# One of twelve blocks of w2 laid as four 16-row blocks on 32 partitions and loaded by eight four-row transfers, in a one-token transformer block

## The chip, the cores and the metric

One core of a Trainium2 chip runs the kernel. The metric is the device time of one execution in microseconds (us), given as the median of several runs. All times inside the execution count from the start of the profiled span.

## The reference, cut to what matters

One token x (640 values) goes through a transformer block whose layer norms are modulated by a condition c: attention over a cache of 8192 positions with 32 heads of 192, then a feed-forward part with squared ReLU.

```python
mod = silu(c) @ w_mod                      # 6 vectors: sa, ca, ga, sb, cb, gb
h = layernorm(x) * (1 + ca) + sa
x = x + ga * attention(h)                  # wq, k_cache, v_cache, wo
h = layernorm(x) * (1 + cb) + sb
r = relu(h @ w1 + b1) ** 2                 # 1536 values
x = x + gb * (r @ w2 + b2)                 # w2: 1536 x 640
```

Everything is 32-bit float. The caches hold nearly all of the 452 MB that are read.

## The kernel before, in words

The kernel streams HBM through three large buffers, each 128 partitions by 14208 floats (`slot`). For each head h, `load_k` brings the keys, with a piece of wq or wo behind them in the same transfer, and `load_v` brings the values. VectorE (DVE) multiplies the keys by the query (`keys`, L201) and sums the products with GpSimd's help (L203 to L205), `softmax` turns the scores into weights, and TensorE (PE) applies them to the values (`values`, L240). A new transfer is issued when the buffer that it overwrites has been used.

Behind the last head come the weights of the rest, all issued by SyncE (SP), whose queue issues in the order of the program: the second part of wm1 (L312), w1 in two pieces (L315), gb, which is the last sixth of w_mod (L316), and w2 in five pieces (`W2_CUT`, L319). w1 and gb share one buffer and take the place of the last head's keys. w2 takes another buffer, that of the last head's values, so it can be issued once PE has applied them. w2 has 1536 rows: they lie as 12 blocks, each of 128 partitions by 640 columns (`FB = 12`); the pieces hold 6, 3, 1, 1 and 1 blocks.

Every transfer signals its landing on one of eight semaphores, DMAHW0 to DMAHW7, which are dealt out in turn along the program. An issue that takes a semaphore whose earlier transfer isn't known to have landed waits for that landing first, and the queue behind it waits with it.

The end of the program is one chain: `project`, `attend` and the second layer norm give hT2; 20 matmuls (L343) make ps_f from w1; DVE adds the bias, applies ReLU and squares (L346 to L348) and transposes the result to fT; 20 matmuls make mods from gb; `WARM = 2` rounds of four matmuls whose result nobody reads follow (L355); then 48 matmuls (L363) sum fT with w2 into ps_y, one block after another as the pieces land; DVE multiplies and adds (L366, L367) and SP stores out_y (L368). A 32-bit matmul appears as two matmul and two weight-load records in the profile, so these 48 matmuls are 96 pairs there.

At the start, `spread` lays the biases out for DVE (L88, L90) while PE computes the first query.

Of the kernel before, what the change touches and what calls it, by code (L numbers as in the profile page):

```python
# [8 lines left out]
F32 = mybir.dt.float32  # L9
# [4 lines left out]
P = 128  # L14
D = 640
# [3 lines left out]
FF = 1536  # L19
G = 4  # L20
DG = D // G
FG = FF // G
KB = DG // 32
FB = FG // 32
PW = 2 * DH
E = 8
ED = 64
# [9 lines left out]
WITHOUT_W = (1, H - 2)  # L37
WITH_W = tuple(h for h in range(H) if h not in WITHOUT_W)
W1_CUT = ((0, 3), (3, 2))
W2_CUT = ((0, 6), (6, 3), (9, 1), (10, 1), (11, 1))  # L40
WARM = 2
EPS = 1e-5


@with_exitstack
def block_kernel(ctx: ExitStack, tc: tile.TileContext, kw, ky, vc, wm0, wm1, w1, gb, w2, out):
    nc = tc.nc
    const = ctx.enter_context(tc.tile_pool(name="const", bufs=1))
    strm = ctx.enter_context(tc.tile_pool(name="strm", bufs=3))
    work = ctx.enter_context(tc.tile_pool(name="work", bufs=2))  # L50
# [3 lines left out]
    def slot(name):  # L54
        return strm.tile([P, SLOT], F32, tag="slot", name=name, bufs=3)
# [16 lines left out]
    wm0_t = slot("wm0_t")  # L72
    nc.sync.dma_start(wm0_t[:, :wm0.shape[1]], wm0)

    small = const.tile([P, 2 * KB + FB + KB], F32, name="small")
    nc.vector.tensor_copy(small, wm0_t[:, KB * 2 * D + WQ:wm0.shape[1]])  # L76
    x_c, c_c, bbc = small[:, :KB], small[:, KB:2 * KB], small[:, 2 * KB:]

    def columns(src, n, name, pool=const, **how):

        t = pool.tile([P, n // 32, 32], F32, name=name, **how)
        nc.vector.transpose(t.rearrange("p b r -> p (b r)"), src)
        return t

    def spread(src, n, name):

        t = work.tile([P, FB + KB, 32], F32, name=name + "_c", tag="spread", bufs=1)
        nc.vector.tensor_copy(t[:, :n], src[:, :, None].to_broadcast([P, n, 32]))  # L88
        r = const.tile([P, 32 * n], F32, name=name)
        nc.vector.transpose(r, t[:, :n].rearrange("p b r -> p (b r)"))  # L90
        return r
# [38 lines left out]
    mods = const.tile([P, 6, DG], F32, name="mods")  # L130
# [144 lines left out]
    def gather():  # L275
# [3 lines left out]
        for g in range(G):  # L279
            nc.tensor.matmul(att_t[0][32 * g:32 * (g + 1), :DG], ident[:, 32 * (g // 2):32 * (g // 2) + 1].to_broadcast([P, 32]),  # L280
                             att_s[:, DG * (g % 2):DG * (g % 2 + 1)], start=True, stop=False)

    x_t = spread(x_c, KB, "x_t")
    bbt = spread(bbc, FB + KB, "bbt")
    for h in range(H):
        i = h // 2
        if h:
# [18 lines left out]
        p = softmax(h, sc)  # L306
# [4 lines left out]

    nc.sync.dma_start(wm1_t[:, WO + KB * D:WO + KB * 3 * D], wm1[:, WO + KB * D:])  # L312
    w1_t = slot("w1_t")
    for b0, n in W1_CUT:
        nc.sync.dma_start(w1_t[:, b0 * FF:(b0 + n) * FF], w1[:, b0 * FF:(b0 + n) * FF])  # L315
    nc.sync.dma_start(w1_t[:, KB * FF:KB * (FF + D)], gb)  # L316
    w2_t = slot("w2_t")
    for b0, n in W2_CUT:
        nc.sync.dma_start(w2_t[:, b0 * D:(b0 + n) * D], w2[:, b0 * D:(b0 + n) * D])  # L319
    gb_t = w1_t[:, KB * FF:KB * (FF + D)].rearrange("p (b n) -> p b n", b=KB)  # L320
    w1_t = w1_t[:, :KB * FF].rearrange("p (b n) -> p b n", b=KB)
    w2_t = w2_t[:, :FB * D].rearrange("p (b n) -> p b n", b=FB)

    project(NPAIR - 1)
# [25 lines left out]

    next(mod(5, 1, gb_t))
    idle = psum.tile([P, 512], F32, tag="sm", name="ps_warm", bufs=2)
    for k in range(WARM):
        for g in range(G):
            nc.tensor.matmul(idle[32 * g:32 * (g + 1)], ones[:, :32], w1_t[:, k, :512], start=True, stop=True)  # L355
    gb2 = const.tile([P, DG], F32, name="gb2")
    nc.vector.tensor_mul(gb2, mods[:, 5], bbt[:, FG:])
    nc.vector.tensor_add(x1, x1, gb2)

    py = psum.tile([P, 512], F32, tag="q", name="ps_y", bufs=2)  # L360
    for b in range(FB):
        for g in range(G):
            nc.tensor.matmul(py[32 * g:32 * (g + 1), :DG], fT[:, b], w2_t[:, b, DG * g:DG * (g + 1)],  # L363
                             start=(b == 0), stop=(b == FB - 1))
    y = const.tile([P, DG], F32, name="y")
    nc.vector.tensor_mul(y, py[:, :DG], mods[:, 5])  # L366
    nc.vector.tensor_add(y, y, x1)  # L367
# [43 lines left out]
```

## Time and profile before

| what | value |
|---|---|
| median of 3 runs | 1057.85 us (1057.68 to 1058.02) |
| profiled execution | 1057.63 us |
| its span | 1055.8 us |
| DVE busy | 831.4 us (79%) |
| PE busy | 451.2 us (43%) |
| GpSimd (POOL) busy | 194.7 us (18%) |
| ScalarE (ACT) busy | 33.4 us (3%) |
| HBM read | 451.82 MB, mean 428 GB/s over the span |
| mean granted TensorE clock | 0.696 of full speed |

Read it from the bottom up: the 16 DMA engines are busy in nine tenths or more of nearly every slice of the span, while no compute engine is. "SPq" in a row means SP's queue: the time of an issue is what SP spends on it, and the data land later.

### The profile page before, as it was taken

How to read it: one execution, taken by the hardware profiler on the slowest of the kernel's cores; microseconds unless marked ns; L12 is line 12 of the kernel's file. 1: busy time of each engine (PE TensorE's matmuls, PEld its weight loads, DVE VectorE, ACT ScalarE, POOL GpSimd, SP SyncE). 2: the span in 40 equal slices, each digit the busy share in tenths (PEclk: the TensorE clock that was granted, in tenths of full speed). 3: DMA queues.
4: the chain of work that ended last, by engine and by line, in shares of the span. 5: the costliest groups of instructions: out<-in, count | busy, mean ns of one | idle time of the engine just before them, and what ended most of it. 6: DMA issues, size and time to landing. Idle time of an engine off the chain costs nothing.

```text
span 1055.8 us, 5623 instructions
## 1 busy us (share of the span) xinstructions
PE 451.2 (43%) x2324; PEld 143.5 (14%) x2324; DVE 831.4 (79%) x409; ACT 33.4 (3%) x88; POOL 194.7 (18%) x72
## 2 busy tenths in 40 slices
PE   3235443344543344363334534335453334545446
PEld 1101111011111111020111111101111111111113
DVE  2886878978787987878888687987878798789963
ACT  1000000000000000000000000000000000000000
POOL 0211112211212221212221212221211221122110
PEclk9667656776665777666577666666666676666769
DMA  9999999999999999999999999999999999999997
GB/s 403 439 434 424 436 436 426 443 424 435 433 435 426 442 424 439 431 433 426 435 432 439 428 436 427 434 437 433 428 435 430 431 436 432 433 429 431 426 423 306
DMA packets 11409, 452.18 MB, mean 428 GB/s; under 512 B 1268, under 2 KB 1272, under 8 KB 1784
## 3 DMA queue, kind: packets, MB, share of 16 engines
q1 hardware_dynamic: 11384, 451.83, 99.3%
q8 instruction: 18, 0.29, 0.1%
q14 instruction: 7, 0.06, 0.0%
HBM read 451.82 MB, written 0.00 MB: 428 GB/s over the span
## 4 chain that ended last, share of the span: by engine, by line
DMA 42%; DVE 39%; PE 17%; ACT 1%; issue 1%; SPq 0%; DVEq 0%; ACTq 0%
DMA k<-in_kw 36%; DVE k L201 21%; PE ps_o L240 14%; DVE sc L204 12%; DVE sc L205 5%; DMA k<-in_ky 3%; DMA w_t<-in_w 2%; DMA wm_t<-in_wm 1%; ACT p L228 1%; PE ps_sum L97 1%; PE ps_mx L220 1%; PE ps_mod L140 1%; PE ps_q L181 0%; DVE nm L222 0%; DVE mp L218 0%
## 5 line engine op out<-in xcount | busy, mean ns | idle before, releaser
L201 DVE TENSOR_TENSOR k<-k,qb 128x6144 f32<-128x6144 f32 (+1 forms) x66 | 419.7, 6359 | 152.3 <-DMA k<-in_kw 148.0
L203 POOL TENSOR_TENSOR k<-k 128x1344 f32<-128x1344 f32 (+1 forms) x66 | 194.0, 2940 | 821.0 <-DVE k L201 443.9
L240 PE MATMUL ps_o<-v,p 128*32 128x512 f32 x1536 | 291.9, 734 | 17.2 <-ACT p L228 17.2
L204 DVE TENSOR_REDUCE sc<-k 128x18 f32<-128x3456 f32 (+1 forms) x66 | 240.5, 3644 | 4.3
L220 PE MATMUL ps_mx<-ident,mp 128*128 128x128 f32 x32 | 15.2, 474 | 421.7 <-DVE mp L218 421.7
L267 PE MATMUL att_a<-k,oT 128*32 128x320 f32 x180 | 49.5, 719 | 118.3 <-DVE oT L262 117.1
L205 DVE TENSOR_REDUCE sc<-k 128x14 f32<-128x1344 f32 (+1 forms) x66 | 99.0, 1500 | 0.0
L240 PEld LDWEIGHTS ps_o<-v,p 128*32 128x32 f32 x1536 | 68.7, 132 | 216.6 <-issue 194.3
L220 PEld LDWEIGHTS ps_mx<-ident,mp 128*128 128x128 f32 x32 | 5.8, 182 | 448.2 <-DVE mp L218 427.2
L181 PE MATMUL ps_q<-k,hR 128*128 128x384 f32 x150 | 52.4, 496 | 1.7 <-DMA k<-in_kw 1.7
L228 ACT ACTIVATE p<-sc,nm 128x256 f32<-128x256 f32 x32 | 16.2, 508 | 759.9 <-DVE nm L222 496.4
L267 PEld LDWEIGHTS att_a<-k,oT 128*32 128x32 f32 x180 | 13.7, 161 | 140.8 <-DVE oT L262 120.7
L181 PEld LDWEIGHTS ps_q<-k,hR 128*128 128x128 f32 x150 | 27.3, 190 | 29.9 <-issue 14.0
L254 DVE SCALAR_TENSOR_TENSOR om<-ps_o,r,mask 96x512 f32<-96x512 f32 x32 | 23.9, 747 | 7.0 <-PE ps_o L240 5.8
L222 DVE TENSOR_REDUCE nm<-ps_mx 128x1 f32<-128x128 f32 x32 | 9.3, 292 | 18.2 <-PE ps_mx L220 18.2
L256 DVE TENSOR_REDUCE os<-om 96x64 f32<-96x512 f32 x32 | 21.8, 682 | 1.1
L97 PE MATMUL ps_sum<-sp,ones 128*128 128x2 f32 x32 | 9.4, 364 | 17.2 <-ACT p L228 17.2
L140 PE MATMUL ps_mod<-wm_t,silu 128*32 128x320 f32 (+1 forms) x120 | 10.5, 503 | 14.5 <-DVE silu L128 14.5
L183 ACT ACTIVATE qb<-ps_q 128x384 f32<-128x384 f32 x16 | 7.8, 490 | 196.3 <-PE ps_q L181 196.3
L97 PEld LDWEIGHTS ps_sum<-sp,ones 128*128 128x128 f32 x32 | 8.0, 312 | 21.9 <-ACT p L228 21.9
L76 DVE COPY small<-wm_t 128x27 f32<-128x27 f32 x1 | 0.2, 179 | 11.1 <-DMA wm_t<-in_wm 11.1
L145 DVE COPY mods<-ps_mod 128x320 f32<-128x320 f32 (+1 forms) x4 | 1.6, 398 | 8.9 <-PE ps_mod L140 8.9
(77 smaller groups left out, 86.7 us busy)
## 6 DMA issues: line engine op xcount, KB each, us to landing
k<-in_kw SPq DMA_DIRECT2D x29, 7104.0 KB, 27.8
v<-in_vc SPq DMA_DIRECT2D x32, 6144.0 KB, 22.1
k<-in_ky SPq DMA_DIRECT2D x1, 6144.0 KB, 30.6
k<-in_ky SPq DMA_DIRECT2D x2, 3072.0 KB, 21.3
k<-in_kw SPq DMA_DIRECT2D x3, 1536.0 KB, 15.3
wm_t<-in_wm SPq DMA_DIRECT2D x1, 4173.5 KB, 12.6
wm_t<-in_wm SPq DMA_DIRECT2D x1, 3200.0 KB, 29.3
wm_t<-in_wm SPq DMA_DIRECT2D x1, 2560.0 KB, 18.4
```

The source lines that it names most:

```text
L97: nc.tensor.matmul(ps[:, :n], ones, src, start=True, stop=True)
L181: nc.tensor.matmul(ps[:, :PW], hR[:, b], w[:, b], start=(b == 0), stop=(b == KB - 1))
L201: nc.vector.tensor_mul(pr, pr, q[:, None, :].to_broadcast([P, n, DH]))
L203: nc.gpsimd.tensor_add(half, half, pr[:, m:, DH // 2:])
L204: nc.vector.tensor_reduce(s[:, :m], pr[:, :m], axis=AX.X, op=ALU.add)
L205: nc.vector.tensor_reduce(s[:, m:], half, axis=AX.X, op=ALU.add)
L220: nc.tensor.transpose(ps[:, :P], mp.to_broadcast([P, P]), ident)
L228: nc.scalar.activation(p, sc[:, :, None].to_broadcast([P, NPOS, 32 // E]), AF.Exp, bias=nm, accum_out=sp[:, h % 2:h % 2 + 1])
L240: nc.tensor.matmul(ps_t[h][32 * g:32 * (g + 1)], p[:, E * j:E * (j + 1)].rearrange("p e r -> p (e r)"), t[:, j, g], start=(j == 0), stop=( ...
L254: nc.vector.scalar_tensor_tensor(om[:n], ps_t.pop(h)[:n].rearrange("p (d e) -> p d e", e=E), r2[:n, a:a + 1], mask[:n, None, :].to_broadca ...
L256: nc.vector.tensor_reduce(os_[:n, a], om[:n], axis=AX.X, op=ALU.add)
L267: nc.tensor.matmul(att_a[32 * g:32 * (g + 1), :2 * DG], oT[:, 32 * j:32 * (j + 1)], w[:, j, 2 * DG * g:2 * DG * (g + 1)], start=(i == 0 an ...
```

## The change

The last of the 12 blocks of w2 leaves the main array. Its 128 rows lie as four blocks (`XB = 4`) of 32 rows, on partitions 0 to 15 and 32 to 47, in a region of their own behind w1 and gb in w1's buffer. They come in eight transfers of 4 rows, each row 2560 floats (10 KB); transfer k goes to partitions p, p+4, p+8 and p+12 with p = 32 * (k // 4) + k % 4. The region is zeroed first by GpSimd. The feed-forward columns are regrouped to match: two of the four groups make 416 columns, two make 352. The eight transfers stand between gb and the main w2 in SP's program. PE multiplies the four small blocks first and the 11 main blocks behind them, and one round of unused matmuls goes.

```diff
-FB = FG // 32
+FB = 11
+XB = 4
+XR = 16
+FX = FB + XB
+FN = (FB * 32 + XB * XR, FB * 32 + XB * XR, FB * 32, FB * 32)
...
-W2_CUT = ((0, 6), (6, 3), (9, 1), (10, 1), (11, 1))
-WARM = 2
+W2_CUT = ((0, 6), (6, 2), (8, 1), (9, 1), (10, 1))
+WARM = 1
...
-    bbt = spread(bbc, FB + KB, "bbt")
+    bbt = spread(bbc, FX + KB, "bbt")
+    f = work.tile([P, FX * 32], F32, name="f", tag="spread", bufs=1)
+    nc.vector.memset(f[:, FB * 32:], 0.0)
...
     w1_t = slot("w1_t")
+    w2x_t = w1_t[:, KB * (FF + D):KB * (FF + D) + XB * D]
+    nc.gpsimd.memset(w2x_t[:64], 0.0)
     for b0, n in W1_CUT:
         nc.sync.dma_start(w1_t[:, b0 * FF:(b0 + n) * FF], w1[:, b0 * FF:(b0 + n) * FF])
     nc.sync.dma_start(w1_t[:, KB * FF:KB * (FF + D)], gb)
+    for k in range(8):
+        p = 32 * (k // 4) + k % 4
+        nc.sync.dma_start(w2x_t[p:p + XR:4], w2x[k])
     w2_t = slot("w2_t")
     for b0, n in W2_CUT:
         nc.sync.dma_start(w2_t[:, b0 * D:(b0 + n) * D], w2[:, b0 * D:(b0 + n) * D])
...
-            nc.tensor.matmul(pf[32 * g:32 * (g + 1), :FG], hT2[:, b], w1_t[:, b, FG * g:FG * (g + 1)],
+            nc.tensor.matmul(pf[32 * g:32 * (g + 1), :FN[g]], hT2[:, b], w1_t[:, b, F0[g]:F0[g] + FN[g]],
                              start=(b == 0), stop=(b == KB - 1))
-    f = work.tile([P, FG], F32, name="f", tag="spread", bufs=1)
-    nc.vector.tensor_add(f, pf[:, :FG], bbt[:, :FG])
+    n = FB * 32
...
+    nc.vector.tensor_add(f[:, :n], pf[:, :n], bbt[:, :n])
+    nc.vector.tensor_add(further(f[:64, n:], 32), further(pf[:64, n:FN[0]], XR), further(bbt[:64, n:32 * FX], 32))
...
+    for x in range(XB):
+        for g in range(G):
+            nc.tensor.matmul(py[32 * g:32 * (g + 1), :DG], fT[:64, FB + x], w2x_t[:64, x, DG * g:DG * (g + 1)],
+                             start=(x == 0), stop=False)
     for b in range(FB):
         for g in range(G):
             nc.tensor.matmul(py[32 * g:32 * (g + 1), :DG], fT[:, b], w2_t[:, b, DG * g:DG * (g + 1)],
-                             start=(b == 0), stop=(b == FB - 1))
+                             start=False, stop=(b == FB - 1))
```

The change also moves the waits on SP's queue. This is the queue before, from the second part of wm1 (in_wm) to the store of the result. In these rows w_t is the buffer of w1, gb or w2, a wait on DMAHW with its number is for the landing of the last transfer that took that semaphore, and _49 belongs to the program's name.

```order
L312 DMA wm_t<-in_wm 128x6400
L315 DMA w_t<-in_w 128x4608 [waits DMAHW1_49,DMAHW2_49,DMAHW0_49,DMAHW3_49,DVE_49,PE_49]
L315 DMA w_t<-in_w 128x3072
L316 DMA w_t<-in_gb 128x3200
L319 DMA w_t<-in_w 128x3840 [waits DMAHW5_49,PE_49]
L319 DMA w_t<-in_w 128x1920
L319 DMA w_t<-in_w 128x640 [waits DMAHW4_49]
L319 DMA w_t<-in_w 128x640
L319 DMA w_t<-in_w 128x640 [waits DMAHW6_49]
L368 DMA out_y<-y 4x160 [waits DMAHW7_49,DVE_49]
```

The semaphores go round: the second part of wm1 has DMAHW6, the two pieces of w1 have DMAHW7 and DMAHW0, gb has DMAHW1, and the five pieces of w2 have DMAHW2 to DMAHW6. The store takes DMAHW7 again. The same place on SP's queue with the change:

```order
L323 DMA w_t<-in_w 128x3072
L324 DMA w_t<-in_gb 128x3200
L327 DMA w_t<-in_w2x 4x2560 [waits Pool_49]
L327 DMA w_t<-in_w2x 4x2560
L327 DMA w_t<-in_w2x 4x2560 [waits DMAHW4_49]
L327 DMA w_t<-in_w2x 4x2560 [waits DMAHW5_49]
L327 DMA w_t<-in_w2x 4x2560 [waits DMAHW6_49]
L327 DMA w_t<-in_w2x 4x2560 [waits DMAHW7_49]
L327 DMA w_t<-in_w2x 4x2560 [waits DMAHW0_49]
L327 DMA w_t<-in_w2x 4x2560 [waits DMAHW1_49]
L330 DMA w_t<-in_w 128x3840 [waits DMAHW2_49,PE_49]
L330 DMA w_t<-in_w 128x1280 [waits DMAHW3_49]
```

The eight small transfers take DMAHW2 to DMAHW7, DMAHW0 and DMAHW1. The sixth, seventh and eighth wait for the landing of w1's first piece, of its second piece and of gb; the first piece of the main w2 stands behind them.

On PE the last part of the program changes from the first of these to the second (ps_warm is the unused product, ps_y the sum with w2):

```order
L355 MATMUL ps_warm<-w_t,ones 32x512 x8
L363 MATMUL ps_y<-w_t,fT 32x160 [waits DMAHW2_49,DVE_49,PE_49]
L363 MATMUL ps_y<-w_t,fT 32x160 x23
L363 MATMUL ps_y<-w_t,fT 32x160 [waits DMAHW3_49]
L363 MATMUL ps_y<-w_t,fT 32x160 x11
```

```order
L372 MATMUL ps_warm<-w_t,ones 32x512 x4
L380 MATMUL ps_y<-w_t,fT 32x160 [waits DMAHW3_49,DMAHW2_49,DMAHW4_49,DMAHW1_49,DMAHW5_49,DMAHW0_49,DMAHW6_49,DVE_49,DMAHW7_49,PE_49,Pool_49]
L380 MATMUL ps_y<-w_t,fT 32x160 x15
L384 MATMUL ps_y<-w_t,fT 32x160 [waits DMAHW2_49]
L384 MATMUL ps_y<-w_t,fT 32x160 x23
L384 MATMUL ps_y<-w_t,fT 32x160 [waits DMAHW3_49]
L384 MATMUL ps_y<-w_t,fT 32x160 x7
```

Sixteen matmuls on the four small blocks now stand ahead of the main blocks and wait for all eight small transfers.

## Rows read from the trace of the kernel before

**Rows 1.** The page: busy us and instructions, DMA by slice, instruction fetches, chain by engine

```profile
PE 451.2 (43%) x2324; PEld 143.5 (14%) x2324; DVE 831.4 (79%) x409; ACT 33.4 (3%) x88; POOL 194.7 (18%) x72
...
DMA  9999999999999999999999999999999999999997
...
q8 instruction: 18, 0.29, 0.1%
...
DMA 42%; DVE 39%; PE 17%; ACT 1%; issue 1%; SPq 0%; DVEq 0%; ACTq 0%
```

**Rows 2.** Chain that ended last, from 1030 us: start us, us, what

```profile
1032.25 19.69 DMA w_t<-in_w
...
1051.98 0.52 PE ps_y L363 x8
```

**Rows 3.** Timeline of SP's queue, from 1017 us: start us, us, engine line

```profile
1017.44 0.80 SPq L315 DMA_DIRECT2D w_t<-in_w  x2
1018.29 0.42 SPq L316 DMA_DIRECT2D w_t<-in_gb  x1
1030.45 2.23 SPq L319 DMA_DIRECT2D w_t<-in_w  x5
1053.24 0.65 SPq L368 DMA_DIRECT2D out_y<-y  x1
```

**Rows 4.** DMA issues, whole span: count, KB each, median us from issue to landing

```profile
wm_t<-in_wm SPq DMA_DIRECT2D x1, 4173.5 KB, 12.6
...
w_t<-in_gb SPq DMA_DIRECT2D x1, 1600.0 KB, 24.3
w_t<-in_w SPq DMA_DIRECT2D x1, 1536.0 KB, 19.8
```

**Rows 5.** The store's line L368 on SP's queue: duration ns, start us

```profile
L368 SPq EVENT_SEMAPHORE  x1: 17/17/17, 1033.9 to 1033.9; - x1
```

**Rows 6.** SP's waits, whole span: us in total, times, longest

```profile
SPq L368 <- DMA w_t<-in_w: 1.2, 1, 1.2
```

**Rows 7.** Timeline of PE, 1040 to 1056 us, idle before in brackets

```profile
1039.65 3.43 PE L343 MATMUL ps_f<-w_t,hT 128*32 128x384 f32 x40 [2.09 <-issue]
1042.87 1.57 PE L140 MATMUL ps_mod<-w_t,silu 128*32 128x160 f32 x40
1044.23 1.93 PE L355 MATMUL ps_warm<-w_t,ones 128*32 128x512 f32 x16
1047.35 1.84 PE L363 MATMUL ps_y<-w_t,fT 128*32 128x160 f32 x48 [1.19 <-DMA w_t<-in_w]
...
1051.98 0.48 PE L363 MATMUL ps_y<-w_t,fT 128*32 128x160 f32 x8 [0.32 <-DMA w_t<-in_w]
```

**Rows 8.** DMA queues, 1054 to 1055.8 us: 40 slices of 0.045 us, packets

```profile
GB/s 0 0 0 0 0 0 0 0 0 0 0 43 14 0 0 0 0 0 0 0 0 0 0 0 0 0 0 0 0 0 0 0 0 0 0 0 0 0 0 0
DMA packets 8, 0.00 MB, mean 1 GB/s; under 512 B 4, under 2 KB 8, under 8 KB 8
```

**Rows 9.** DMA queues, 1037 to 1041 us: packets, MB, share of 16 engines

```profile
q8 instruction: 1, 0.02, 1.7%
```

**Rows 10.** DMA queues, 1049 to 1051.95 us

```profile
q8 instruction: 1, 0.02, 2.3%
```

**Rows 11.** Windows: PE, PEld, DVE, ACT, POOL busy, PEclk, DMA share, GB/s

```profile
1016.00:1020.00 4.00, 1.24 (x7) 0.88 (x11) 1.88 (x4) 1.40 (x3) 0.30 (x1) 0.50 0.86 370
1049.00:1051.00 2.00, 1.48 (x39) 0.87 (x32) 0.00 (x0) 0.00 (x0) 0.00 (x0) 1.00 0.33 122
```

**Rows 12.** Timeline of all engines at the start, 0 to 45 us

```profile
0.73 0.20 POOL masks.py:197 MEMSET ident<- 128x128 f32 x1 [0.29 <-POOLq L404]
24.30 0.72 DVE L88 COPY bbt_c<-small 128x544 f32<-128x544 f32 x1
25.05 0.74 DVE L90 STREAM_TRANSPOSE bbt<-bbt_c 128x544 f32<-128x544 f32 x1
30.24 6.56 DVE L201 TENSOR_TENSOR k<-k,qb 128x6144 f32<-128x6144 f32 x1 [4.44 <-DMA k<-in_kw]
```

More of the change, by code (lines that the diff above doesn't have):

```diff
@@ L21 @@
 DG = D // G
-FG = FF // G
 KB = DG // 32
-FB = FG // 32
+FB = 11
[3 more added lines that the diff above has]
+FN = (FB * 32 + XB * XR, FB * 32 + XB * XR, FB * 32, FB * 32)
+F0 = tuple(sum(FN[:g]) for g in range(G))
 PW = 2 * DH
@@ L39, with block_kernel @@
 W1_CUT = ((0, 3), (3, 2))
-W2_CUT = ((0, 6), (6, 3), (9, 1), (10, 1), (11, 1))
-WARM = 2
+W2_CUT = ((0, 6), (6, 2), (8, 1), (9, 1), (10, 1))
+WARM = 1
 EPS = 1e-5
 @with_exitstack
-def block_kernel(ctx: ExitStack, tc: tile.TileContext, kw, ky, vc, wm0, wm1, w1, gb, w2, out):
+def block_kernel(ctx: ExitStack, tc: tile.TileContext, kw, ky, vc, wm0, wm1, w1, gb, w2, w2x, out):
     nc = tc.nc
@@ L73, in block_kernel @@
     nc.sync.dma_start(wm0_t[:, :wm0.shape[1]], wm0)
-    small = const.tile([P, 2 * KB + FB + KB], F32, name="small")
+    small = const.tile([P, 2 * KB + FX + KB], F32, name="small")
     nc.vector.tensor_copy(small, wm0_t[:, KB * 2 * D + WQ:wm0.shape[1]])
@@ L85, in spread @@
     def spread(src, n, name):
-        t = work.tile([P, FB + KB, 32], F32, name=name + "_c", tag="spread", bufs=1)
+        t = work.tile([P, FX + KB, 32], F32, name=name + "_c", tag="spread", bufs=1)
         nc.vector.tensor_copy(t[:, :n], src[:, :, None].to_broadcast([P, n, 32]))
@@ L321, in block_kernel @@
     w1_t = w1_t[:, :KB * FF].rearrange("p (b n) -> p b n", b=KB)
+    w2x_t = w2x_t.rearrange("p (b n) -> p b n", b=XB)
     w2_t = w2_t[:, :FB * D].rearrange("p (b n) -> p b n", b=FB)
@@ L342, in block_kernel, with further @@
         for g in range(G):
-            nc.tensor.matmul(pf[32 * g:32 * (g + 1), :FG], hT2[:, b], w1_t[:, b, FG * g:FG * (g + 1)],
+            nc.tensor.matmul(pf[32 * g:32 * (g + 1), :FN[g]], hT2[:, b], w1_t[:, b, F0[g]:F0[g] + FN[g]],
                              start=(b == 0), stop=(b == KB - 1))
-    f = work.tile([P, FG], F32, name="f", tag="spread", bufs=1)
-    nc.vector.tensor_add(f, pf[:, :FG], bbt[:, :FG])
+    n = FB * 32
+    def further(t, r):
+        return t.rearrange("p (x r) -> p x r", r=r)[:, :, :XR]
+    nc.vector.tensor_add(f[:, :n], pf[:, :n], bbt[:, :n])
+    nc.vector.tensor_add(further(f[:64, n:], 32), further(pf[:64, n:FN[0]], XR), further(bbt[:64, n:32 * FX], 32))
     nc.vector.tensor_scalar(f, f, 0.0, None, op0=ALU.max)
     nc.vector.tensor_mul(f, f, f)
-    fT = columns(f, FG, "fT", work, tag="om", bufs=1)
+    fT = columns(f, 32 * FX, "fT", work, tag="om", bufs=1)
     next(mod(5, 1, gb_t))
@@ L356, in block_kernel @@
     gb2 = const.tile([P, DG], F32, name="gb2")
-    nc.vector.tensor_mul(gb2, mods[:, 5], bbt[:, FG:])
+    nc.vector.tensor_mul(gb2, mods[:, 5], bbt[:, 32 * FX:])
     nc.vector.tensor_add(x1, x1, gb2)
     py = psum.tile([P, 512], F32, tag="q", name="ps_y", bufs=2)
+    for x in range(XB):
+        for g in range(G):
+            nc.tensor.matmul(py[32 * g:32 * (g + 1), :DG], fT[:64, FB + x], w2x_t[:64, x, DG * g:DG * (g + 1)],
+                             start=(x == 0), stop=False)
     for b in range(FB):
@@ L385, in column @@
         return a(v).reshape(G, n, 32).transpose(0, 2, 1).reshape(P, n)
+    ff = np.stack([F0[g] + np.arange(FB * 32).reshape(FB, 32) for g in range(G)])
+    fx = np.stack([F0[g] + FB * 32 + np.arange(XB * XR).reshape(XB, XR) for g in range(2)])
+    b1 = np.zeros((G, 32, FX), np.float32)
+    b1[:, :, :FB] = a(B_b1)[ff].transpose(0, 2, 1)
+    b1[:2, :XR, FB:] = a(B_b1)[fx].transpose(0, 2, 1)
+    w2 = a(B_w2)[ff.transpose(0, 2, 1)].reshape(P, FB * D)
+    w2x = a(B_w2)[fx.transpose(0, 2, 1)].reshape(2, XR // 4, 4, XB * D).transpose(0, 2, 1, 3).reshape(8, XR // 4, XB * D)
     wq = a(A_wq).reshape(G, KB, 32, NPAIR, PW).transpose(3, 0, 2, 1, 4).reshape(NPAIR, P, WQ)
@@ L397 @@
         "wm0": np.concatenate([rows(wm[:, :2 * D], KB), wq[0], column(A_x, KB), column(c, KB),
-                               column(B_b1, FB), column(B_b2, KB)], axis=1),
+                               b1.reshape(P, FX), column(B_b2, KB)], axis=1),
         "wm1": np.concatenate([wo[-1], rows(wm[:, 2 * D:3 * D], KB), rows(wm[:, 3 * D:5 * D], KB)], axis=1),
@@ L401 @@
         "gb": rows(wm[:, 5 * D:], KB),
-        "w2": rows(B_w2, FB),
+        "w2": np.ascontiguousarray(w2),
+        "w2x": np.ascontiguousarray(w2x),
     }
```

## The prediction

> **What bounds the kernel now.** I read the page first, for who is busy: the DMA engines fill nine tenths of nearly every slice, and the chain that ended last is mostly DMA and DVE [rows 1]. The change touches only the last 40 us, so I then read the chain from 1030 us on: one transfer of w2, from the end of its issue at 1032.25 to its landing at 1051.94, then 0.52 us of matmuls [rows 2] and what little follows them. PE's timeline says the same from the other side: from 1047.35 on every group of ps_y begins when a piece of w2 has landed [rows 7]. So the end is set by the landing of the last piece of w2, and my question is when that piece lands after the change.
>
> What SP issues when comes from its timeline: w1 at 1017.44, gb at 1018.29, w2's five pieces from 1030.45 [rows 3]. How long each is under way comes from the list of issues: gb lands 24.3 us after its issue [rows 4], at 18.29 + 24.3 = 1042.6. The second piece of w1, issued some 0.4 us before gb, lands after 19.8 us [rows 4], at about 1037.7. So w2 is issued 12 us before gb has landed. The transfers behind each other keep the DMA engines fed, and w2 needs 1051.94 - 1042.6 = 9.34 us from gb's landing to its own: 3840 KB at 411 KB per us. That is my price for streaming.
>
> **The wait that the change adds.** In the program's order, the eighth small transfer takes the semaphore of gb and waits for gb's landing; the sixth and seventh wait for the two pieces of w1. The main w2 stands behind them on the same queue. That such a wait really holds SP is to be seen before: the store of out_y takes the semaphore of w1's first piece, and SP's marker of line L368 ends at 1033.9 [rows 5], a wait of 1.2 us for a transfer into w_t [rows 6] after w2's last issue. There nothing was queued behind it that mattered. Now the sixth small transfer goes at about 1033.9, the seventh at 1037.7 and the eighth at 1042.65, and the first piece of the main w2 behind it, 12.7 us later than the 1030.45 of before. By then gb, the last large transfer in the queue, is in: the DMA engines run dry, and w2 starts cold.
>
> **The sum, from gb's landing at 1042.6.**
> - SP: 0.05 us to react, then the eighth small transfer's issue. Ordinary issues take 0.42 us, the store with its four rows 0.65 [rows 3]. I take 0.55, near the one with four rows. The main w2 is issued at 1043.2.
> - The cold start: what a transfer needs from issue to landing beyond its streaming. No row has it for w2, so I bound it. Below: out_y, issued at 1053.24, moves its first packets in the twelfth slice after 1054, at 1054.5 [rows 8], so 1.3 us without any landing. Above: the very first load, 4173.5 KB in 12.6 us [rows 4], less 4173.5 / 411 = 10.15, so 2.45. I take 2.4, because that load is the nearest kind: 128 rows from HBM into idle engines.
> - Streaming 11 of 12 blocks: 9.34 x 11/12 = 8.56 us. Here lies what the change removes, 0.78 us. The pieces behind the first are issued while it streams and cost nothing more; their cover is its 4.7 us.
> - PE's instruction fetches: transfers of 0.02 MB on queue q8. One in a window of 2.95 us takes 2.3% of 16 engines, which is 1.1 us of one engine [rows 10]; the one in the window from 1037 takes the same [rows 9]. Before, the later one came in the window from 1049 [rows 10], where two thirds of the engines' time was free [rows 11], and it cost next to nothing. The page has 18 such packets, and 2324 matmuls and as many weight loads on PE [rows 1]: one fetch for every 129 pairs of load and matmul, if they are all PE's, as the count suggests. Counting from the fetch before ps_f: before, 40 pairs of ps_f, 40 of ps_mod and 16 of ps_warm [rows 7] put the next one near the 33rd pair of ps_y. Now ps_warm has 8 pairs and the small blocks 32, so it comes near the 9th pair of the main w2. These run when six blocks have landed, near 1043.2 + 2.4 + 4.7 = 1050.3, in the middle of the stream. The data of one engine wait for it, and a transfer has landed only when all its shares have. Between 0 and 1.1 us; I take 0.9, since it falls into the stream.
>
> Landing of the last piece: 1043.2 + 2.4 + 8.56 + 0.9 = 1055.06, against 1051.94: 3.1 us later.
>
> **What else the change adds.** The 32 pairs on the small blocks run after 1045 and are over before the main w2 has six blocks in; without that cover they would cost about 1.2 us (48 pairs take 1.84 [rows 7]). The chain from ps_f to fT grows by a small addition and a quarter more columns, about 0.4 us, and ends before 1046, under the same cover. GpSimd's zeroing holds the first small transfers: 128 columns take 0.20 us [rows 12], 20 times that is at most 4 us, so until 1021.5, and the sixth waits for 1033.9 anyway. At the start, the longer bias layout (1.46 us for 544 columns, so 0.26 more) and a memset end near 26.2 us; DVE's next operation waits for the first keys until 30.24 [rows 12]. None of these reaches the end. The last four matmuls take 0.48 us with the clock granted in full [rows 7, 11]; PE now idles some 4 us before the main blocks, and after the idle stretches before 1017 the granted clock was 0.50, its lower level [rows 11]. At that level they would take twice as long: 0 to 0.5 us, and I take 0.1, since groups at work stand between that idle time and the last one.
>
> The sum is +3.2 us against the profiled execution's 1057.63. The median of the runs is 0.2 us above that execution, so I forecast **1061.0 us** for the median.
>
> On the cold start the Trainium skill says (DMA: Bandwidth & Descriptors, "Anatomy of one DMA") that a transfer pays a fixed cost of about 2.0 us whatever its size, most of it until the write is confirmed; it was fitted there for transfers issued by GpSimd. By it the sum would be 1060.6 instead of 1061.0. The first load's 2.45 us is above it, and I go by that row.
>
> **The rivals.**
> 1. *The queue doesn't run dry.* If the waits were over earlier than I read them, say because an earlier transfer's landing satisfied them, the change would do only what its data say: the last engine has 1/12 of w2 less to move, 0.78 us, so 1057.1. It decides if the main w2 is issued before about 1042.6 - 2.4 = 1040.2. For it: the eight small transfers carry only 320 KB. Against it: SP's marker at 1033.9 [rows 5], exactly such a wait. Chance 0.05.
> 2. *A cheap restart.* The cold start is that of out_y, 1.3 us, the small issue takes 0.42, and the fetch falls outside the stream: 1042.6 + 0.5 + 1.3 + 8.56 = 1052.96, or +1.0 us, 1058.9. For it: the eighth small transfer goes ahead and may wake the engines. Against it: the row of the first load, and PE's count. Chance 0.17.
> 3. *The small transfers pile up.* A transfer of four rows moves in few packets: out_y's 4 rows are 8 packets, four of them tiny [rows 8]. If all eight go to the same four engines, each of these carries 80 KB, 3.1 us at a sixteenth of 411 KB per us, where an even spread gives 0.78. On engines that end gb early this hides. On one that ends gb last at 1042.6 it lasts until 1045.7, about 0.6 us into the stream, and the first piece of the main w2 waits for the first small one too, 0.4 us. Then 1062.0. No row tells which engines end gb last. Chance 0.13.
>
> The third is also what a rule of the Trainium skill gives (the same page, "Why a DMA increments its semaphore by 16 and not by 1"): a transfer issued by SP uses as many engines as divide its outer dimension, up to 16, and the lowest-numbered ones, so all eight would use the same four. No row here names an engine, and eight packets for four rows agree with the first half of it.
>
> **How the numbers follow.** My own case has the rest, 0.65, and by its bounds reaches from 1059.9 to 1062.0. A measurement of this kernel can tell about 0.2%, 2.1 us, from no change, so slower begins at 1060.0. Slower: nearly all of my case and the third rival, 0.79 together. Rivals 1 and 2 lie within 0.2%, and with the low edge of my case this makes 0.20. Faster by more would take a gain of over 2.1 us, more than the 0.78 that is there: 0.01. The range from 1059.0 to 1063.0 holds my case, the third rival and the upper part of the second, and leaves out the first.
>
> **What would show it.** Right: SP's first issue of the main w2 near 1043.2; a stretch of about 2 us after 1043 in which the DMA engines are nearly idle; the first main group of ps_y near 1050; one q8 packet within the stream; the last group near 1055. Wrong: an issue of the main w2 before 1040, or no idle stretch (rival 1); 1.5 us or less from that issue to the first data at full rate (rival 2); a stream that runs on for a few slices with few engines busy (rival 3). A difference that arises before 1017 us would also prove me wrong, since up to there I count nothing.

## The result, and the profile after

| what | before | after |
|---|---|---|
| median | 1057.89 us (6 runs, 1057.67 to 1058.64) | 1062.81 us (6 runs, 1062.14 to 1063.56) |
| ratio after / before | | 1.0046, 95% interval 1.0036 to 1.0057 |
| profiled execution | 1057.63 us | 1062.74 us |
| its span | 1055.8 us | 1061.0 us |

The change makes the kernel slower by 4.9 us. The forecast was 1061.0 us, with a range from 1059.0 to 1063.0: the sign and the range held, the size fell short by 1.8 us.

SP's timeline of the changed kernel, from 1015 us on (start, duration, line, operation), answers to [rows 3]:

```profile
1019.18 0.81 SPq L323 DMA_DIRECT2D w_t<-in_w  x2
1020.04 0.43 SPq L324 DMA_DIRECT2D w_t<-in_gb  x1
1021.49 22.94 SPq L327 DMA_DIRECT2D w_t<-in_w2x  x8
1044.53 2.48 SPq L330 DMA_DIRECT2D w_t<-in_w  x5
```

The eight small transfers take SP 22.94 us, and the main w2 goes out at 1044.53, where before it went out at 1030.45 [rows 3]. What SP waited for in them stands in the view of waits (total us, times, longest):

```profile
SPq L327 <- DMA w_t<-in_w: 8.0, 2, 4.9
SPq L327 <- DMA wm_t<-in_wm: 5.1, 1, 5.1
SPq L327 <- DMA w_t<-in_gb: 4.8, 1, 4.8
```

They are the landings of four earlier transfers whose semaphores are taken again: wm1, the two pieces of w1 and, last, gb. The chain of waits now runs through these (start, duration, what), where before it was one transfer of w2 [rows 2]:

```profile
1020.04 23.80 DMA w_t<-in_gb
...
1043.85 0.58 SPq L327
...
1046.48 10.70 DMA w_t<-in_w
...
1057.23 0.52 PE ps_y L384 x8
```

From 1020.04 it is gb; then the issue of the eighth small transfer, which starts 0.01 us after gb has landed; then the main w2 to its landing at 1057.18. The windows show what the engines did meanwhile (columns as in [rows 11]):

```profile
1042.00:1044.00 2.00, 2.00 (x30) 1.24 (x26) 0.00 (x0) 0.00 (x0) 0.00 (x0) 1.00 0.08 32
1044.00:1045.00 1.00, 1.00 (x21) 0.55 (x15) 0.00 (x0) 0.00 (x0) 0.00 (x0) 1.00 0.03 10
...
1048.00:1050.00 2.00, 1.29 (x32) 1.00 (x32) 0.95 (x4) 0.00 (x0) 0.00 (x0) 1.00 1.04 445
...
1052.00:1053.00 1.00, 1.00 (x20) 0.73 (x16) 0.00 (x0) 0.00 (x0) 0.00 (x0) 0.50 0.95 376
...
1054.00:1055.00 1.00, 0.94 (x28) 0.52 (x22) 0.00 (x0) 0.00 (x0) 0.00 (x0) 0.88 0.93 369
1055.00:1056.00 1.00, 0.94 (x24) 0.38 (x16) 0.00 (x0) 0.00 (x0) 0.00 (x0) 1.00 0.08 31
1056.00:1057.00 1.00, 0.57 (x12) 0.16 (x8) 0.00 (x0) 0.00 (x0) 0.00 (x0) 1.00 0.05 18
```

Read the second number from the right, the DMA share. For three microseconds it is 0.08 and 0.03: the queue ran dry. It began to before gb had landed: a window ahead of these, first in the kernel before and then, a microsecond shorter, in the changed one, reads

```profile
1040.00:1043.00 3.00, 3.00 (x44) 1.51 (x40) 0.00 (x0) 0.00 (x0) 0.00 (x0) 1.00 0.98 416
1040.00:1042.00 2.00, 0.16 (x4) 0.19 (x8) 1.60 (x5) 0.00 (x0) 0.00 (x0) 1.00 0.49 193
```

The trace keeps the time of each step by which a large transfer's semaphore rises. There are 16, as many as engines, and I read each as one engine's share landing. By them seven engines are through with gb by 1039.55 and the last one at 1043.84. Before, w2 was queued behind gb, and the seven that were through first, by 1038.36, had ended w2 by 1047.74. From 1048 on the changed kernel's share is near 1. The stream then ends abruptly, from 0.93 to 0.08 and 0.05, where one engine of sixteen is 0.06: for nearly two microseconds a single engine is still at work. Before, the share fell slowly, to 0.33 between 1049 and 1051 [rows 11]. What else moved in that stretch stands in the DMA queues from 1051 to 1054 us (packets, MB, share of 16 engines):

```profile
q8 instruction: 1, 0.02, 2.0%
```

2.0% of 16 engines over 3 us is 0.96 us of one engine: PE's instruction fetch, as the prediction's count of such packets took it, and as the variants with fewer and with more matmuls below bear out. PE's timeline ends so:

```profile
1051.67 4.42 PE L384 MATMUL ps_y<-w_t,fT 128*32 128x160 f32 x72 [2.08 <-DMA w_t<-in_w]
1056.42 0.48 PE L384 MATMUL ps_y<-w_t,fT 128*32 128x160 f32 x8 [0.33 <-DMA w_t<-in_w]
1057.23 0.48 PE L384 MATMUL ps_y<-w_t,fT 128*32 128x160 f32 x8 [0.33 <-DMA w_t<-in_w]
```

The 72 pairs take 4.42 us, partly at the lower clock level (0.50 in the window from 1052), but PE has caught up by 1056.09 and the last two groups wait for data at full clock, as before [rows 7].

### The profile page after: what moved, and what is told of

It is laid out like the page before. It is cut to its first block, busy times and chain, and to the rows that moved or that the text cites. A ratio compares the mean times of both kernels' runs of the same rounds, so it can differ in the third digit from the quotient of the medians.

```text
span 1061.0 us, 5671 instructions
## 1 busy us (share of the span) xinstructions
PE 454.6 (43%) x2340; PEld 145.6 (14%) x2340; DVE 831.8 (78%) x411; ACT 33.4 (3%) x88; POOL 197.1 (19%) x73
## 4 chain that ended last, share of the span: by engine, by line
DMA 44%; DVE 39%; PE 16%; ACT 1%; issue 1%; SPq 0%; DVEq 0%; ACTq 0%
DMA k<-in_kw 36%; DVE k L205 21%; PE ps_o L244 13%; DVE sc L208 12%; DVE sc L209 5%; DMA k<-in_ky 3%; DMA w_t<-in_gb 2%; DMA wm_t<-in_wm 1%; DMA w_t<-in_w 1%; ACT p L232 1%; PE ps_sum L101 1%; PE ps_mx L224 1%; PE ps_q L185 1%; PE ps_mod L144 1%; DVE nm L226 0%
## 5 line engine op out<-in xcount | busy, mean ns | idle before, releaser
L144 PE MATMUL ps_mod<-wm_t,silu 128*32 128x320 f32 (+1 forms) x120 | 11.6, 545 | 14.9 <-DVE silu L132 14.9
L80 DVE COPY small<-wm_t 128x30 f32<-128x30 f32 x1 | 0.2, 182 | 11.5 <-DMA wm_t<-in_wm 11.5
```

The source lines that it names most:

```text
L144: nc.tensor.matmul(ps[32 * g:32 * (g + 1), :n * DG], e[:, b:b + 1].to_broadcast([P, 32]), wb[:, :, DG * g:DG * (g + 1)], start=(b == 0), s ...
```

## The experiments

My theory after the result: the held SP queue makes the DMA engines run dry; what the forecast missed is a later gb and a dearer fetch. The rivals: the eight transfers cost time by their number or by their few rows; the layout costs time in itself (matmuls on 64 partitions, more DVE work); or the changed program starts later.

### Hold without data: eight and six tiny transfers in the kernel before

```diff
     nc.sync.dma_start(w1_t[:, KB * FF:KB * (FF + D)], gb)
+    spare_t = w1_t[:, KB * (FF + D):KB * (FF + D) + 16]
+    for k in range(8):
+        p = 32 * (k // 4) + k % 4
+        nc.sync.dma_start(spare_t[p:p + 16:4], w2[p:p + 16:4, :16])
```

The kernel before, with eight transfers of four rows of 64 bytes that nobody reads. With `range(6)` it is the second variant.

> The kernel before with eight transfers of 4 rows of 64 bytes between gb and w2; nothing reads them. Theory of the held queue: the first piece of w2 is issued only after gb has landed, near 1043.3, the DMA engines run dry, and w2 pays 0.7 us of issues, a cold start of 2.5 us and a fetch of 1.1 to 1.6 us: 4.3 to 4.8 us more than before, 1062.2 to 1062.7 us. Rival, the new layout (its matmuls, its wider DVE work, its 10 KB rows on few engines) is what costs: nothing of it is here, so 1057.9 us within 0.5.

> The same with six of them. Theory of the held queue: the first piece of w2 then waits for the second piece of w1 alone, near 1037.7, some 5 us before gb has landed, and the rest of w2 is issued while that piece is under way; the engines never run dry, so 1057.9 us within 0.6. If small transfers cost by their number, and not by the wait, six of them give three quarters of what eight give, near 1061.3 us. Rival, the new layout: 1057.9 us.

Eight: 1061.8 us (1060.61 to 1062.18), ratio 1.0036 (1.0024 to 1.0049), 0.4 us under the range of the held queue and far over the rival's. Six: 1057.92 us, ratio 1.0005 (0.9996 to 1.0014). SP's timeline and a window of the variant with eight:

```profile
1019.53 23.62 SPq L320 DMA_DIRECT2D w_t<-in_w  x8
1043.25 2.39 SPq L323 DMA_DIRECT2D w_t<-in_w  x5
```

```profile
1042.00:1044.00 2.00, 2.00 (x32) 1.01 (x28) 0.00 (x0) 0.00 (x0) 0.00 (x0) 1.00 0.00 0
```

and of the variant with six:

```profile
1018.84 15.73 SPq L320 DMA_DIRECT2D w_t<-in_w  x6
1037.73 6.69 SPq L323 DMA_DIRECT2D w_t<-in_w  x5
```

```profile
1042.00:1044.00 2.00, 2.00 (x48) 1.50 (x44) 0.74 (x2) 0.00 (x0) 0.00 (x0) 1.00 1.05 415
```

Six hold SP until 1037.7, the landing of w1's second piece. gb is still under way then, w2's first pieces join the queue behind it, the share stays at 1.05, and nothing is lost. Two more hold SP until gb is in, the share is 0.00, and 4 us are lost with 2 KB moved. So the loss comes from which landing SP is held for: not from the number of small transfers, the bytes or the layout.

One thing differs from the changed kernel. Here the chain of waits ends with PE:

```profile
1043.25 7.10 DMA w_t<-in_w
...
1050.48 6.33 PE ps_y L367 x96
```

96 pairs take 6.33 us without a pause, at a granted clock of 0.50 from 1050 to 1056, after PE had idled 3.3 us. The last piece lands at 1055.13 by the steps of its semaphore, 3.2 us later than before; with 0.56 us behind it, as in the other chains, PE would have ended near 1055.7 instead of 1056.82. So some 1.1 us of this variant's loss is PE at its lower level, and the rest is the later data.

### Keeping PE at work until w2 comes

```diff
-WARM = 2
+WARM = 5
```

In the variant with eight tiny transfers: 40 warming pairs instead of 16.

> tiny8 with 40 warming matmuls in place of 16, so that PE works on until about 1050 (24 more at 1.93/16 us each, 2.9 us) and idles at most a microsecond before the first blocks of w2. Clock theory of tiny8's end (PE idled 3.3 us, its clock was granted at 0.50 from 1050 to 1056, and 96 matmuls took 6.3 us, past the landing of the last piece): the clock stays at 1.00, each group of ps_y waits for its piece, the last group ends about 0.5 us after the last landing, and the time is 0.6 to 1.2 us under tiny8's 1061.8, so 1060.6 to 1061.2. Rival, the landing of the last piece sets tiny8's end whatever PE's clock: 1061.5 to 1062.1. In both, SP stays held until 1043 and the queue runs dry: neither gives a time under 1060.

1062.29 us (1062.18 to 1062.7), ratio 1.0045 (1.0032 to 1.0057): slower than both expectations. The chain of waits and the DMA queues from 1047.5 to 1050 us say why:

```profile
1045.40 11.23 DMA w_t<-in_w
1056.63 0.04 issue
1056.67 0.52 PE ps_y L367 x8
```

```profile
q8 instruction: 1, 0.02, 2.4%
```

The end is now the landing of the last piece, at 1056.63, and no longer PE. Fifteen of its sixteen steps are over by 1055.27, the sixteenth comes 1.36 us behind them. Without the extra pairs no q8 packet lies between 1047.5 and 1050, and one lies between 1053.5 and 1056; the 24 added pairs moved the fetch to the front of the stream. It also delayed the first piece, so PE idled 3.2 us all the same and the clock fell to 0.50 between 1052 and 1055. The test of the clock therefore failed. What it shows is that 24 pairs of idle matmuls are enough to put the fetch into the stream, and that two ends lie close together: PE at its lower clock level (1056.8 without), and one delayed engine (1057.19 with).

### No fetch in the stream

```diff
-    for x in range(XB):
+    for x in range(0):
...
-    for b in range(FB):
+    for b in range(8, FB):
...
-                             start=False, stop=(b == FB - 1))
+                             start=(b == 8), stop=(b == FB - 1))
```

The changed kernel without the matmuls on the four small blocks and on the first eight main blocks, 24 of 120 pairs left (48 of 60 matmuls are left out, not 44 as the expectation has it). All data still come.

> The changed kernel without the products of the four small blocks and of the first eight main blocks: 44 of 60 matmuls are left out, all transfers stay. Then PE does not reach the point at which it fetches its next instructions while w2 streams. Theory of the fetch: the last piece lands 1.2 to 1.6 us earlier, 1061.2 to 1061.6 us. Rival, the fetch harms nothing and the cold start alone is longer than I took it: 1062.8 us.

1061.39 us (1060.92 to 1061.43), ratio 1.0034 (1.0021 to 1.0047). The main w2 goes out at 1044.05. No q8 packet lies between 1049 and 1056, and the windows show no tail of one engine:

```profile
1054.00:1055.00 1.00, 1.00 (x16) 0.20 (x8) 0.00 (x0) 0.00 (x0) 0.00 (x0) 0.50 0.37 146
1055.00:1056.00 1.00, 0.93 (x12) 0.20 (x8) 0.00 (x0) 0.00 (x0) 0.00 (x0) 0.50 0.00 0
```

Data end under 11 us after the main issue; in the changed kernel, with the fetch, they go on for over 11.5 us. The sixteen steps of the last piece lie within 0.47 us, none late, and it lands at 1055.14, 11.09 us after the main issue; with the fetch that takes 12.65 and 12.54 us in the two profiles of the changed kernel. So the tail comes with the fetch, which costs 1.45 to 1.56 us at the landing. The whole gain doesn't reach the end, since PE at its lower level takes over: 24 pairs, of which the last 8 take 0.81 us.

### Undoing the hold alone: the small transfers on GpSimd's queue

```diff
-        nc.sync.dma_start(w2x_t[p:p + XR:4], w2x[k])
+        nc.gpsimd.dma_start(w2x_t[p:p + XR:4], w2x[k])
```

> The changed kernel with one word different: the eight small transfers are issued by GpSimd instead of SP, so SP has nothing that waits for gb's landing and the semaphores of SP's queue are used as before. Held-queue theory: SP issues the main w2 near 1030.5 to 1034, no stretch after 1042 with the DMA share under 0.3, and the time is 1057.5 to 1060.0 (at best 0.8 us under before, since 1/12 of w2 is off the last engines; at worst 2 us over, where the small transfers make a tail on four engines, as in mix2). Rival, the small transfers themselves are the cost, whoever issues them (number, few rows, few partitions): 1061.5 or more, as the changed kernel.

1059.57 us (1059.47 to 1059.85), ratio 1.0018 (1.0009 to 1.0027), 3.2 us under the changed kernel's first runs and 2.4 us under its later ones. SP's timeline and the windows:

```profile
1032.42 2.23 SPq L330 DMA_DIRECT2D w_t<-in_w  x5
```

```profile
1042.00:1044.00 2.00, 2.00 (x30) 1.28 (x26) 0.00 (x0) 0.00 (x0) 0.00 (x0) 1.00 0.97 408
1044.00:1046.00 2.00, 1.98 (x34) 1.03 (x30) 0.62 (x2) 0.00 (x0) 0.00 (x0) 1.00 0.96 398
```

The dry stretch is gone with the hold, everything else of the change being there but the queue on which the small transfers run. 1.9 us over before remain. w1 is issued 1.45 us later than before, at 1018.89, but the end hangs on one engine: fifteen steps of w2's last piece are over by 1051.89, where before the whole had landed at 1051.94, and the sixteenth comes at 1053.82. At the landing of w1's first piece one engine is 2.8 us behind the next already (1034.43 and 1037.25), while GpSimd's transfers are under way (their steps lie between 1025.97 and 1038.57). The eleven runs lie within 0.4 us, so the 1.9 us belong to the variant and not to a single execution. That GpSimd's transfers put this engine behind would fit; no run shows it.

### The transfers themselves: two of 16 rows

```diff
-    for k in range(8):
-        p = 32 * (k // 4) + k % 4
-        nc.sync.dma_start(w2x_t[p:p + XR:4], w2x[k])
+    for k in range(2):
+        nc.sync.dma_start(w2x_t[32 * k:32 * k + XR], w2x[k])
```

> The changed kernel, but the four small blocks come in two transfers of 16 rows. Theory of the held queue: no issue waits longer than for the first two pieces of w1 and the first piece of the main w2 goes near 1030.5 as before, so 1057.9 us, at most 1.2 us more if an instruction fetch falls into the stream. Rival, the new layout: its matmuls and its DVE work are all here, so 1061 to 1063 us.

> The kernel with two 16-row transfers once more, unchanged. If the start belongs to the program, w1 is issued at 1017.5 give or take 0.2 again; if to the execution, most likely over 0.3 us away from that. The crowded partitions show in either case: gb lands two to three us later than in the kernel before, with the DMA share near 1 and under 300 GB/s between 1042 and 1045, and the time is 1061 to 1063.

1062.06 us, ratio 1.0042 (1.0029 to 1.0054), and 1062.11 us, ratio 1.0042 (1.0029 to 1.0054), in the repeat. I expected the loss to go with the hold, and that was wrong. SP is free and issues the first piece of the main w2 at 1030.40, but gb lands some 3 us later than before. PE's timeline of the first run shows who waits for it, before the matmuls that need gb (L144):

```profile
1045.83 1.56 PE L144 MATMUL ps_mod<-w_t,silu 128*32 128x160 f32 x40 [2.54 <-DMA w_t<-in_gb]
```

And the windows show engines that are busy and move little:

```profile
1042.00:1044.00 2.00, 1.28 (x14) 0.33 (x6) 0.65 (x2) 0.00 (x0) 0.00 (x0) 1.00 1.03 161
1044.00:1045.00 1.00, 0.00 (x0) 0.00 (x0) 0.93 (x2) 0.00 (x0) 0.00 (x0) 1.00 0.88 223
```

At a share of 1.03 they move 161 GB/s, where the streams elsewhere move over 400. The second run shows the same, 186 GB/s at a share of 1.22. The wait for gb isn't on the chain that ended last: that is w2, whose first piece also lands late, at 1051.60, and then PE without a pause.

```profile
1030.40 21.20 DMA w_t<-in_w
...
1051.64 4.77 PE ps_y L383 x88
```

So this variant trades the hold for another cost, and says nothing about the hold.

### The same block on 32 partitions spread over all 128

```diff
-XR = 16
-FN = (FB * 32 + XB * XR, FB * 32 + XB * XR, FB * 32, FB * 32)
+XR = 8
+FN = (FB * 32 + XB * XR,) * G
...
-    for k in range(8):
-        p = 32 * (k // 4) + k % 4
-        nc.sync.dma_start(w2x_t[p:p + XR:4], w2x[k])
+    nc.sync.dma_start(w2x_t[::4], w2x)
```

Four small blocks again, of 8 rows in each group of 32 partitions, so on partitions 0, 4, 8 to 124, in one transfer; zeroing, bias, addition and matmuls follow the rows.

> The changed kernel with the block's 128 rows on partitions 0, 4, 8 ... 124 (8 rows of each block in each of the four groups) in one transfer of 32 rows. In the version with two transfers of 16 rows to partitions 0 to 15 and 32 to 47 nothing held SP, and yet gb landed some 3 us late. Theory of the crowded partitions: rows that many engines write to few neighbouring partitions slow these engines; spread over all partitions they don't, so gb lands near 1042.6 and the whole is 1057.3 to 1059.2 us. Rival, the layout or its matmuls cost by themselves: 1061 to 1062.5 us.

1058.57 us (1058.44 to 1058.81), ratio 1.0008 (0.9999 to 1.0017). SP issues the main w2 at 1030.70, and the same window reads:

```profile
1042.00:1044.00 2.00, 1.82 (x35) 0.83 (x28) 0.61 (x2) 0.00 (x0) 0.00 (x0) 1.00 0.95 401
```

The same 320 KB in one transfer of 32 rows: with the partitions spread, 401 GB/s instead of 161. The cut into transfers differs too, so the packet records help: the median time of a row of 10 KB is 0.39 us here, and the same in the changed kernel, where four rows at a time go to the crowded partitions. In the two runs with sixteen rows at a time it is 0.78 and 0.83 us, the longest 1.27. So rows slow each other when many at once go to few partitions. And the rest of the change, 32 more pairs, the longer bias, the addition and the zeroing, costs nothing that this measurement tells from none, since all of it is here: the medians are 0.7 us apart, and the interval reaches from 0.1 us less to 1.8 us more.

### Other orders

**Early.** The small blocks get a buffer of their own, one small transfer goes ahead of each `load_v` of heads 4 to 11, and the eight behind gb go.

```diff
+        if 4 <= h < 12:
+            p = 32 * ((h - 4) // 4) + h % 4
+            nc.sync.dma_start(w2x_t[p:p + XR:4], w2x[h - 4])
         load_v(h)
```

> The changed kernel, but the small blocks have a buffer of their own and the eight transfers of 4 rows are issued one by one with heads 4 to 11. All of the new layout's matmuls, DVE work and bias columns are here; between gb and the main w2 stands nothing. Theory of the held queue: the first piece of the main w2 goes near 1030.5 and the end has 0.8 us less to stream, so 1056.9 to 1058.7 us (the upper end if an instruction fetch falls into the stream). Rival, the layout costs by itself (as the 1062.06 us of the version with two transfers would have it): 1061 to 1062.5 us.

1059.46 us (1059.28 to 1059.92), ratio 1.0017 (1.0008 to 1.0026), between the two ranges expected. There is no hold: the main w2 goes out at 1034.07, and gb is under way. The end is 2 us later than before because all before it is: w1 goes out at 1020.78, 3.3 us later. From there to the last landing, at 1053.81, it takes 33.0 us against 34.5 before. The eleven runs lie within 0.7 us, so the later start belongs to this variant; what in it costs that wasn't tried.

**Interleaved.** Four small transfers go ahead of gb, one behind it, three behind the second piece of the main w2. In the cut, `small` and `main` issue the transfers named.

```diff
+    small(range(0, 4))
     nc.sync.dma_start(w1_t[:, KB * FF:KB * (FF + D)], gb)
+    small(range(4, 5))
+    main(W2_CUT[:2])
+    small(range(5, 8))
+    main(W2_CUT[2:])
```

> The changed kernel with SP's order altered: four small transfers, gb, one small transfer, the first two pieces of the main w2, three small transfers, the rest. All eight stay transfers of 4 rows. Theory of the held queue: the first main piece waits for w1's first piece, near 1034, the second for w1's second, near 1038, and the rest is issued while 6 us of work are queued; no dry stretch, 1057.1 to 1059.2 us. Theory of the pile-up: four engines carry 60 KB more than their share, and the one of them that is latest ends 2.3 us later than it did, so up to 1060.2 us, with a tail in which few engines work. Theory of the layout: 1061 to 1063 us.

1063.77 us, ratio 1.0058 (1.0045 to 1.007), the slowest of all and over every range expected, though the main w2 starts at 1034.5. The chain of waits:

```profile
1039.81 11.48 DMA w_t<-in_w2x
1051.29 0.35 issue
1051.63 2.36 PE ps_y L390 x32
1053.99 4.37 PE ps_y L394 x88
```

The last small transfer stands behind eight blocks of w2 and lands 11.5 us after its issue. PE takes the small blocks first, so all 120 pairs wait for it, and run at 0.50 until 1056.

**Interleaved, small blocks later.** As above, but PE takes eight main blocks, the small ones, then the last three.

> The version with SP's order altered, with PE's order altered too: eight main blocks, the four small ones, the last three. That version took 1063.77 us though its pieces were issued in time; PE began on the small blocks at 1051.63 and worked without a pause until 1058.37, long with the granted clock at 0.50. Theory: there PE was the bound, because the small blocks stood first and their last transfer came late on the four crowded engines. Now the main blocks are done as they land and the end is the landing of the last transfer, 1059.5 to 1061 us. If that order is harmless: 1063.8 us.

1059.82 us (1059.4 to 1060.3), ratio 1.0018 (1.0009 to 1.0027): 3.95 us back for an order of matmuls. The DMA share is 0.15 from 1050 to 1052 and 0.05 from 1052 to 1054, a tail on few engines. The last piece lands at 1054.07, but PE, at 0.50 until 1052, works without a pause from 1049.05 to 1055.32, so here too PE is the end, by some 0.7 us.

### The changed kernel again

> The changed kernel once more, unchanged. In its first profile SP issued w1 at 1019.18, in that of before at 1017.44; with two 16-row transfers, which has the very same instructions up to there, at 1017.54. If the later start belongs to the changed program, w1 is issued at 1019.2 give or take 0.2 again. If it belongs to the single execution, it lies anywhere between 1017.4 and 1020, most likely over 0.3 us away from 1019.18, and the span moves with it. The held queue shows in either case: the main w2 near 1043 to 1045, and the time 1061.5 to 1063.5.

1062.01 us (5 runs, 1061.96 to 1062.12), ratio 1.0041 (1.0027 to 1.0054). w1 goes out at 1017.79 this time, not 1019.18. So 1.4 us of the first profile's later start are not the program's. In the repeat of two transfers of 16 rows it went out at 1017.83 instead of 1017.54, a distance of 0.29 that decides for neither of the two cases expected. Whether the change moves the start by a few tenths stays open: the profiles of the changed layout, Early apart, have it between 1017.54 and 1019.18, those of the layout before between 1017.43 and 1018.21. The chain of waits:

```profile
1018.65 24.41 DMA w_t<-in_gb
...
1043.08 0.58 SPq L327
...
1043.76 8.66 DMA w_t<-in_w
1052.42 0.04 issue
1052.46 4.55 PE ps_y L384 x88
```

The main w2 goes out 0.70 us after gb's landing at 1043.06. PE's 88 pairs, in part at the lower level, end at 1057.01, 0.2 us later than the last landing alone would have it (1056.30 and 0.52): both ends coincide.

## Why the prediction was right, and where it was off

Its terms beside the two profiles of the changed kernel. In each, fifteen of the sixteen steps of the last piece's semaphore come together and one late; the term of the fetch is the distance.

| term | forecast | first profile | again |
|---|---|---|---|
| gb's landing | 1042.6 | 1043.84 | 1043.06 |
| SP: to the main w2's issue | 0.6 | 0.69 | 0.70 |
| cold start and 11 blocks: to fifteen steps | 2.4 + 8.56 = 10.96 | 1055.62 - 1044.53 = 11.09 | 1054.90 - 1043.76 = 11.14 |
| fetch: to the sixteenth | 0.9 | 1057.18 - 1055.62 = 1.56 | 1056.30 - 1054.90 = 1.40 |
| last landing | 1055.06 | 1057.18 | 1056.30 |
| profiled execution | +3.2 | +5.11 | +4.36 |

- **The held queue.** Right, by its place, its cause (the semaphores of w1 and gb taken again) and its end. The variants with eight and six tiny transfers and with GpSimd's queue show it. Rival 1, a queue that doesn't run dry, is refuted by the share of 0.08 and 0.03.
- **SP's 0.6.** The small issue takes 0.58, where 0.55 was taken, and SP's steps around it 0.1 in place of 0.05.
- **Cold start.** The sum of 10.96 was 0.13 to 0.18 short. With the forecast's own 8.56 for streaming the cold start is 2.53 and 2.58, nearer the first load's 2.45 [rows 4] than anything else; by the same sum it is 2.53 without the fetch, and with eight tiny transfers, where all 12 blocks follow, 2.54 and 2.46. In the first profile's packet records w2's first data start 1.0 to 1.5 us after the issue, and each engine's first packet takes 0.8 to 1.6 us where most of the later ones take 0.57. By the Trainium skill's 2.0 us (DMA: Bandwidth & Descriptors, "Anatomy of one DMA") it would have come out half a microsecond too low; the measurement decides. Rival 2, a cheap restart, is refuted.
- **The fetch, 0.9: mis-sized.** It falls into the stream as forecast, but costs 1.40 and 1.56, above the bound of 1.1 that I had taken from the packet's own time. What the engine does in the other 0.4 to 0.6 us no row shows. That the count put it in the right place is partly luck: by the same count the later fetch of before would come at the 33rd pair of ps_y, near 1048.6, and its packet starts at 1050.15, when some 60 pairs are done. And one thing made the cost certain that I had not seen: after a dry stretch all engines start w2 together and end together, in the two profiles fifteen of them within 0.43 and 0.62 us. Whichever engine the fetch hits is the last one. Before, the engines ended spread out, as the falling share shows [rows 11]: seven by 1047.74, eight between 1049.84 and 1050.71, one at 1051.94. The fetch of [rows 10] could hit one with time to spare. The earlier one [rows 9] did not: it lies in gb's stream, and the last engine, level with the others at the landing of w1's second piece (1037.46 and 1037.56), is 1.23 us behind them at gb's (1041.39 and 1042.62) and still at the end. So the kernel before pays for one fetch as well; it is hidden in the 24.3 us that I took for gb.
- **gb's landing, 1042.6: not counted.** I held everything up to gb's landing for unchanged. The first profile has gb 1.24 later, the second 0.46. In the first profile gb was issued 1.75 us later already, in the second 0.36; by the repeat, 1.4 us of that is the execution's and not the change's. The fetch in gb's stream has a part in it too: it puts the last engine 1.59 and 1.01 us behind, where before it was 1.23. gb, the fetch and the two smaller terms make the last landing 2.1 us later than forecast in the first profile and 1.2 us in the second; the medians are 1.8 and 1.0 us over the forecast.
- **The 0.78 of streaming.** It holds from gb's landing on, where it stands in the sum. It is no gain of the kernel: the 320 KB move ahead of gb's landing instead. With no hold, from w1's issue to the last landing, GpSimd's queue takes 34.9 us and the spread rows 35.1, against 34.5 before. My rival of 1057.1 had no variant that came near it.
- **The clock, 0.1.** PE idled 2.08 us before the main blocks, not some 4. It did fall to its lower level, and had caught up before the last two groups in the first profile. In the second it adds 0.2. Right by its size, but nearer to the path than I thought: in the variant with eight tiny transfers, and in the interleaved ones, PE at that level is the end.
- **Rival 3, the pile-up.** Its price is not seen in the changed kernel: gb takes 23.80 and 24.41 us from its issue, 24.3 before [rows 4]. Its condition, the same four engines for all, fits the steps of the first profile: the data of each of the first seven small transfers land in four, and from one transfer to the next these follow at 0.38 to 0.40 us, the time of one 10 KB row. But three of the four were through with gb by 1039.5 and with seven small rows by 1042.2; the fourth ended its seventh at 1044.86, before w2's first data. In the interleaved orders, where small transfers stand behind main pieces, few engines carry a tail and the time goes there. That agrees with the Trainium skill's rule on the lowest-numbered engines (DMA: Bandwidth & Descriptors, "Why a DMA increments its semaphore by 16 and not by 1"); no row names the engines.
- **The chances.** My own case and rival 3 come to 0.78 together, so slower, which is a little less than both, can't have the 0.79 that I gave it.

Open are what the fetch costs beyond its packet, and why w1 goes out between 1017.4 and 1019.2 in kernels that differ little up to there. The five later runs of the changed kernel lie within 0.16 us, and all of them under the first six; what sets such a group of runs apart wasn't tried. The later groups ran on four different chips, and on these the kernel before took 1057.63 to 1057.83 us.

## What to carry to other kernels

Count the transfers on a queue between an issue and the earlier one whose semaphore it will take: the issue waits for that landing, and so does all that stands behind it. It costs nothing while a large transfer is still under way behind the one waited for, and a cold start, 2.5 us here, when it is the last. Of versions tried, none beats the kernel before; the one that splits w2 at no cost that can be told, 1.0008 (0.9999 to 1.0017), uses one transfer on partitions spread over all 128.

## What had not been expected of the hardware

- Two transfers of 16 rows into partitions 0 to 15 and 32 to 47 slow the DMA engines: 161 and 186 GB/s at a full busy share, and gb 3 us later, for 320 KB. On partitions 0, 4 to 124 it is 401 GB/s, and four rows at a time into the first set take no longer than there, 0.39 us each. The Trainium skill has a rule for this (SBUF — State Buffer, "Door 1: The DMA port swizzle"): a partition's number decides which of 16 ports it is written through, and by its table the first set reaches four of them and the second all sixteen. The trace agrees in direction. A quarter of the ports for 320 KB would be some 3 us instead of 0.8 at the 411 KB per us of the forecast, an estimate by that page; the 3 us of gb are a little more than the difference of 2.3.
- A dry stretch takes away the spread between the engines, so that one fetch of 0.02 MB in the stream behind it costs its full 1.36 to 1.56 us.
- After 3.2 to 3.3 us without work PE ran its next blocks at a granted clock of 0.50, for 3 to 6 us, and in the changed kernel after 2.08 us too; 96 pairs then take 6.33 us, where 48 took 1.84 at full clock [rows 7].
